# Attention start-up and filler of a fused attention and two-layer network kernel: operands of the second pair, products of zeros, filler rate, copies

## The chip, the cores and the metric

The kernel is one program on one core of a Trainium2 chip. The metric is the device time of one execution in microseconds (us), less being better. TensorE runs the matrix products, VectorE and ScalarE read its results out of PSUM, GpSimd works on SBUF, and SyncE issues most DMAs. The times of three runs and one profiled execution are shown.

## The reference, cut to what matters

```
scores = q @ k.T / 8, masked causally, plus min(-(cum_i - cum_j), 0)   # cum = cumsum(max(s, 0))
attn   = softmax(scores);  x = attn @ v        # batch 4, heads 8, sequence 576, head size 64
x = x.reshape(2304, 512)                       # heads side by side
h = x @ w1_in;  x = (h * sigmoid(1.702 h)) @ w1_out          # 512 -> 2048 -> 512
h = x @ w2_in;  out = (P(h) / Q(h)) @ w2_out                 # P cubic, Q quadratic in |h|
```

## The kernel before, in words

The attention works on one pair of heads at a time: 4 batches of 4 pairs. A pair has five units, blocks of 128 query rows t = 0, 1, 4, 2, 3 (block 4 has 64 rows, both heads together), so there are 80 units; the loop of `attention` (L417) counts them as j. A unit is two `unit_scores` (L251 two products per head; L285 on VectorE adds the mask and takes the minimum, L292 on ScalarE the exponential, L304 on GpSimd scales by the reciprocal sum), and, three units later in the first batch and two later after it, `unit_transpose` (products with the identity, L323 to L344, and a copy `pt<-tp` out of PSUM, L324 to L351) and one unit after that `unit_values` (L370, the product with v).

A pair's operands are made by `prep`, which is a generator in two steps: step one transposes k on TensorE (`tk`, L218), step two q (`tq`); each result is split into a high and a low part (L176 on ScalarE, L179 on VectorE), and the high part is copied to the other half of the partitions by a DMA from SBUF to SBUF (L225, `kh<-kh` and `k<-qs`). The rows with the running sum come by L204 from a scratch in DRAM which `store_sums` fills (L113, L115). The loop takes a step of the next pair's `prep` in a pair's first and second unit; in the very first pair `if j` (L437) holds it back, so there the steps come in units j = 1 and j = 2, and j = 5 is the first unit that needs them. The loads of v are `values` (L152, L156); those of the first two pairs are traced ahead of `store_sums` (L413 to L415).

Until j = 23 there is no other work for TensorE: `fill` (L385) then issues `warm` products of zeros (L75, `idle`), three per unit for j below 4 and one per unit after that. From j = 23 on, `fill` interleaves the first fifth of layer one for the batch that is done (`mlp1_first`, L562 and L586), by a credit of FILL / 20 us per unit in three portions; one batch's work comes to 29.6 us in these costs, so at FILL = 33 it is used up after some 18 units of 20 (L434).

The layer's weights are split into two parts by `convert` (L493 to L506: one DMA, then ScalarE, VectorE, GpSimd in turn). Ten of them are emitted at the units in CONV_J, from j = 9 on; up to j = 23 they share one staging buffer, so that each load waits for the GpSimd sum (L504) of the one before.

TensorE's instructions run in the order written. On the other engines and on SyncE's queue a planner sets the order: it takes, of what it thinks ready, what stands first in the program. `COPY_V` lists the (batch, t) whose copies `pt<-tp` go to VectorE; all others go to ScalarE.

Of the kernel before, what the change touches and what calls it, by code (L numbers as in the profile page):

```python
# [41 lines left out]
PACE = 0.5  # L42
AHEAD_F = (5, 6, 7)
AHEAD_J = (35, 39, 43, 47, 51, 55)
FILL = 33.0
AHEAD, AHEAD_0 = 2, 3
COPY_V = ((0, 0), (0, 4))
W2_SLOTS = 7
CONV_J = (9, 12, 15, 18, 20, 22, 24, 26, 28, 30)
CONV = [(f, 0) for f in range(F1)] + [(f, 1) for f in range(F1)]  # L50
# [5 lines left out]
class Fused:  # L56
# [249 lines left out]
    def unit_transpose(self, att, u):  # L306
# [10 lines left out]
        st["pt"] = {}  # L317
        copy = nc.vector.tensor_copy if (b, t) in COPY_V else nc.scalar.copy
        if t == 4:
# [77 lines left out]
    def attention(self, att, mlp):  # L397
        units = [(b, p, t) for b in range(NB) for p in range(NP) for t in (0, 1, 4, 2, 3)]
        n = len(units)
        self.pairs, self.state = {}, {}  # L400
        self.filler, self.credit = iter(()), 0.0
        self.n_bt = 0
        self.cold, self.idle_bank = True, self.bank("T", "idle")
        self.warm(10)
        nprep = iter(())
        self.sums_load(att)
        ld = self.pair_load(att, 0, 0, True)
        self.sums(att)
        for _ in self.prep(att, 0, 0, ld, True):
            pass  # L410
        start = ld["values"]
        ld = self.pair_load(att, 0, 1)
        start()  # L413
        ld["values"]()
        self.store_sums()  # L415
        done = 0
        for j in range(n + AHEAD + 1):  # L417
            i = max(j - (AHEAD_0 if j < 20 else AHEAD), -1)
            for e in range(done, i):
                for _ in self.unit_transpose(att, units[e]):  # L420
                    pass
                self.unit_values(att, units[e - 1])
            done, k = i + 1, i - 1
            self.stg_free = j > 23
            tr = iter(())
            if j < n:
                b, p, t = units[j]
                idx = j % 5
                if idx == 0 and units[j][1:] != (NP - 1, 0) or (idx == 0 and b + 1 < NB):
                    nprep = self.prep(att, *divmod(b * NP + p + 1, NP), ld)  # L430
            if i >= 0 and i < n and units[i][0] and i % 20 == 1:
                self.filler = chain(self.filler, self.mlp1_first(mlp, units[i][0] - 1))
                self.cold = False
            q = FILL / 20  # L434
            if j < n:
                self.unit_scores(att, units[j], 0)
                if j:  # L437
                    next(nprep, None)
            self.fill(q / 3, 1)
            if 0 <= i < n:  # L440
                tr = self.unit_transpose(att, units[i])
                next(tr, None)
            if j < n:
                self.unit_scores(att, units[j], 1)
            self.fill(q / 3, j < 4)
            for _ in tr:
                pass
            if j < n and idx == 4:
                for _ in nprep:
                    pass  # L450
                g = b * NP + p + 2
                if g < NB * NP:
                    ld = self.pair_load(att, *divmod(g, NP))
                    ld["values"]()
            if k >= 0:
                self.unit_values(att, units[k])
            self.fill(q / 3, j < 4)
            if j == AHEAD_J[0]:
                self.stg_n, self.stg_k = 0, 2
                buf = self.stg_slot[:, 2 * STG : 2 * STG + 1024].bitcast(F32R)  # L460
                buf = buf.rearrange("p (i f) -> p i f", i=2)
                self.queue = [
                    lambda f=f, half=half: self.park(buf, 1, f, half)
                    for f in AHEAD_F for half in range(2)
                ]
            if j in COEF_J:
                with self.behind(self.tail):
                    if j == COEF_J[0]:
                        self.coefficients()
                    else:  # L470
                        self.nc.scalar.activation(self.cf[:, 6:8], self.cf[:, 4:6], AF.Abs)
            if j in CONV_J or j in AHEAD_J:
                with self.behind(self.tail):
                    self.emit(1)
        for _ in self.filler:
            pass
# [434 lines left out]
```

## Time and profile before

| | |
|---|---|
| median of 3 runs | 1064.91 us (1062.8 to 1066.14) |
| profiled execution | 1062.4 us, span 1060.6 us |
| TensorE products (PE) busy | 1029.6 us, 97% |
| VectorE (DVE), ScalarE (ACT), GpSimd (POOL) busy | 805.7 us, 722.8 us, 259.4 us |
| mean granted TensorE clock | 0.993 |

The span is that from the first to the last instruction. The attention ends near 328 us; the rest of the kernel is the two layers. The granted clock is a share of full speed, 1.00 for 2.4 GHz and 0.50 for 1.2 GHz; a stretch in between is a mean of the two.

### The profile page before, as it was taken

What the parts mean: (1) busy time and instruction counts of PE and PEld (TensorE: products, weight loads), DVE (VectorE), ACT (ScalarE), POOL (GpSimd) and SP (SyncE); (2) the same over time, 40 slices, a digit from 0 to 9 for tenths busy, and PEclk for the clock granted to TensorE, in tenths of its full rate; (3) what the DMA queues carried; (4) which work ended last, traced back from release to release, by engine and by line L of the source; (5) the groups of instructions that cost most, each with busy time, mean ns of one, the idle gap of its engine ahead of it and who ended that gap; (6) DMA issues with size and microseconds to landing.
All of it is one profiled execution on the core that took longest, in us unless ns stands there. A gap on an engine that the chain in (4) does not pass through costs nothing.

```text
span 1060.6 us, 19849 instructions
## 1 busy us (share of the span) xinstructions
PE 1029.6 (97%) x7073; PEld 942.3 (89%) x7073; DVE 805.7 (76%) x1874; ACT 722.8 (68%) x1668; POOL 259.4 (24%) x321
## 2 busy tenths in 40 slices
PE   6998999999999999998999999999999999999997
PEld 4767998898999899988999999998999999999996
DVE  6787767766644998884379344898998988989886
ACT  6898868978855675563265224787777777777765
POOL 4455734543420000000000000222222222222222
PEclk8999999999999999999999999999999999999999
DMA  8456455543215648995146546100010010100000
GB/s 183 120 153 163 112 148 157 137 138 82 53 46 222 204 160 277 300 305 175 46 125 209 188 124 243 48 30 30 2 47 14 15 46 1 31 30 1 31 1 30
DMA packets 88203, 117.31 MB, mean 111 GB/s; under 512 B 25728, under 2 KB 71808, under 8 KB 86508
## 3 DMA queue, kind: packets, MB, share of 16 engines
q1 hardware_dynamic: 87688, 115.43, 36.3%
q8 instruction: 56, 0.92, 0.4%
q0 software_dynamic: 192, 0.31, 0.2%
q14 instruction: 43, 0.35, 0.1%
q10 hardware_dynamic: 224, 0.30, 0.1%
HBM read 75.08 MB, written 32.05 MB: 101 GB/s over the span
## 4 chain that ended last, share of the span: by engine, by line
PE 73%; DMA 12%; DVE 6%; ACT 5%; issue 2%; POOL 1%; SPq 0%; ACTq 0%; DVEq 0%; POOLq 0%
PE h L562 29%; PE a L727 18%; PE a L586 12%; DMA raw<-in_moe_w_out_dram 5%; PE s L251 5%; PE O L370 4%; PE tp L344 2%; DMA stgA<-in_moe_w_in_dram 2%; DMA raw<-in_moe_w_in_dram 2%; DMA xp<-x 1%; DVE cvx L504 1%; DMA wd<-park 1%; ACT cvx L499 1%; DVE gl L579 1%; DVE cvx L502 1%
## 5 line engine op out<-in xcount | busy, mean ns | idle before, releaser
L710 POOL TENSOR_TENSOR gl<-u,gh 128x384 fp32r<-128x384 f32 x96 | 105.5, 1099 | 625.9 <-DMA x<-st 339.3
L562 PE MATMUL h<-x,u 128*128 128x288 f32 x1536 | 234.5, 298 | 5.3 <-ACT st L600 1.6
L586 PE MATMUL a<-gh,u 128*128 128x288 f32 x1024 | 232.3, 299 | 4.1 <-DVE st L637 3.0
L562 PEld LDWEIGHTS h<-x,u 128*128 128x128 f32 x1536 | 212.8, 188 | 11.2 <-DVE g L574 3.1
L586 PEld LDWEIGHTS a<-gh,u 128*128 128x128 f32 x1024 | 172.4, 188 | 10.2 <-DVE st L637 2.8
L562 PE MATMUL h<-y,u 128*128 128x384 f32 x864 | 166.2, 336 | 0.0
L562 PEld LDWEIGHTS h<-y,u 128*128 128x128 f32 x864 | 153.0, 188 | 6.3
L586 PE MATMUL a<-gl,u 128*128 128x288 f32 x512 | 148.6, 296 | 1.2 <-DVE gl L579 1.2
L727 PE MATMUL a<-u,gh 128*128 128x512 f32 x432 | 114.9, 394 | 0.9 <-ACT gh L708 0.9
L304 POOL TENSOR_SCALAR bt<-bt,sm 128x128 f32<-128x128 f32 (+3 forms) x129 | 71.3, 563 | 113.8 <-DVE sm L301 59.7
L586 PEld LDWEIGHTS a<-gl,u 128*128 128x128 f32 x512 | 96.3, 188 | 2.6 <-DVE gl L579 1.8
L292 ACT ACTIVATE bt<-bt,mn 128x128 f32<-128x128 f32 (+3 forms) x129 | 74.8, 580 | 29.7 <-DVE mn L285 28.1
L727 PEld LDWEIGHTS a<-u,gh 128*128 128x128 f32 x432 | 80.0, 188 | 14.9 <-ACT gh L708 1.7
L285 DVE CUSTOM_DVE_ANT_0 bt<-s,mask 128x128 f32<-128x128 f32 (+3 forms) x129 | 62.3, 483 | 37.1 <-PE s L251 31.2
L573 ACT ACTIVATE g<-h 128x288 f32<-128x288 f32 x128 | 51.1, 405 | 56.8 <-PE h L562 51.9
L576 ACT ACTIVATE gh<-g 128x288 fp32r<-128x288 f32 x128 | 55.7, 442 | 48.0 <-DVE g L574 47.3
L708 ACT ACTIVATE gh<-u 128x384 fp32r<-128x384 f32 x96 | 50.6, 527 | 54.2 <-DVE u L706 53.2
L693 ACT ACTIVATE y<-h,cf 128x384 f32<-128x384 f32 x96 | 55.6, 579 | 38.6 <-PE h L562 38.6
L574 DVE SCALAR_TENSOR_TENSOR g<-g,h 128x288 f32<-128x288 f32 x128 | 56.9, 448 | 32.4 <-ACT g L573 32.1
L251 PE MATMUL s<-k 68*128 68x256 f32 (+2 forms) x192 | 72.5, 382 | 8.7 <-DVE qs L179 4.8
L698 DVE SCALAR_TENSOR_TENSOR y<-s,cf,y 128x384 f32<-128x384 f32 x96 | 59.4, 618 | 24.5 <-ACT s L695 23.5
L706 DVE SCALAR_TENSOR_TENSOR u<-y,u 128x384 f32<-128x384 f32 x96 | 72.7, 757 | 1.1
(115 smaller groups left out, 2014.5 us busy)
## 6 DMA issues: line engine op xcount, KB each, us to landing
raw<-in_moe_w_in_dram SPq DMA_DIRECT2D x24, 512.0 KB
raw<-in_moe_w_out_dram SPq DMA_DIRECT2D x24, 512.0 KB
x<-st SPq DMA_DIRECT2D x64, 144.0 KB
wd<-park SPq DMA_DIRECT2D x36, 256.0 KB
u<-wd SPq DMA_DIRECT2D x8, 1024.0 KB
x2p<-st SPq DMA_DIRECT2D x32, 144.0 KB
xp<-x2p SPq DMA_DIRECT2D x32, 144.0 KB
xp<-x SPq DMA_DIRECT2D x32, 144.0 KB
```

Source lines behind the costliest of these rows:

```text
L251: nc.tensor.matmul(sc[: c1 - c0, :w], lhsT=q[:, c0:c1], rhs=k[:, j0 : j0 + w], start=m == 0, stop=m == 1,)
L285: nc.vector.tensor_tensor_reduce(bt[:, j0 : j0 + w], sc[:, :w], mask, 1.0, 3.0e38 if i == 0 else mn[:, 0:1], ALU.add, ALU.min, mn[:, i : i ...
L292: ex = nc.scalar.activation(bt[:, :n], bt[:, :n], AF.Exp, bias=mn[:, i : i + 1], scale=-1.0, accum_out=sm[:, col : col + 1],)
L304: nc.gpsimd.tensor_scalar(bt[:, :n], bt[:, :n], inv[:, i : i + 1], 1.0, ALU.mult, ALU.mult)
L562: nc.tensor.matmul(ps_tile, lhsT=u[:, wl, kk * P : (kk + 1) * P], rhs=x(xl, kk), start=(n == 0), stop=(n == 3 * KD - 1),)
L574: nc.vector.scalar_tensor_tensor(g[:, :w], g[:, :w], 1.0, h, ALU.add, ALU.mult)
L576: nc.scalar.activation(gh[:, :w], g[:, :w], AF.Copy)
L586: nc.tensor.matmul(acc, lhsT=u[:, wl, d * P : (d + 1) * P], rhs=g[gl], start=(first and i == 0), stop=(last and i == 2),)
L698: nc.vector.scalar_tensor_tensor(y, s, cf[:, 7:8], y, ALU.mult, ALU.add)
L706: last = nc.vector.scalar_tensor_tensor(p, y, 2.0, p, ALU.subtract, ALU.mult)
L710: nc.gpsimd.tensor_tensor(gl, p, gh.bitcast(F32), ALU.subtract)
L727: nc.tensor.matmul(accs[m], lhsT=g[gl][:, m * P : (m + 1) * P], rhs=u[:, wl, :], start=(f == 0 and i == 0), stop=(f == NF - 1 and i == 2),)
```

## The change

It makes four edits in the attention's loop. `store_sums` is traced ahead of the two loads of v, and the second pair's v is loaded in unit 2. The second pair's `prep` takes its steps in units 0 and 1. The first `fill` of a unit issues its product of zeros only for j below 4 or in a pair's first unit; 15 of the 49 products of zeros go (units 4, 6 to 9, 11 to 14, 16 to 19, 21 and 22). The filler's rate is 30 instead of 33 until j = 43. And in the second batch the copies of t = 0, 1 and 4 go to VectorE.

```diff
-FILL = 33.0
+FILL, FILL_1 = 33.0, 30.0
-COPY_V = ((0, 0), (0, 4))
+COPY_V = ((0, 0), (0, 4), (1, 0), (1, 1), (1, 4))
...
         ld = self.pair_load(att, 0, 1)
+        self.store_sums()
         start()
-        ld["values"]()
-        self.store_sums()
...
-            q = FILL / 20
+            q = (FILL_1 if j < 43 else FILL) / 20
             if j < n:
                 self.unit_scores(att, units[j], 0)
-                if j:
-                    next(nprep, None)
-            self.fill(q / 3, 1)
+                next(nprep, None)
+            self.fill(q / 3, j < 4 or j % 5 == 0)
...
+            if j == 2:
+                ld["values"]()
             if k >= 0:
                 self.unit_values(att, units[k])
```

## Rows read from the trace of the kernel before

**Rows 1.** Windows: stretch, length, busy PE PEld DVE ACT POOL, clock, DMA share, GB/s.
```profile
12.50:27.10 14.60, 11.31 (x60) 8.39 (x60) 9.69 (x36) 8.70 (x26) 2.39 (x5) 0.82 0.77 185
27.10:41.80 14.70, 14.70 (x126) 11.35 (x126) 11.05 (x45) 11.12 (x33) 5.20 (x10) 0.88 0.39 96
41.80:56.30 14.50, 13.33 (x128) 10.28 (x126) 12.07 (x45) 12.88 (x37) 7.71 (x11) 1.00 0.54 142
...
83.90:105.00 21.10, 17.48 (x134) 14.75 (x134) 14.71 (x43) 18.16 (x49) 12.16 (x14) 0.95 0.51 130
105.00:163.00 58.00, 58.00 (x508) 52.39 (x506) 40.19 (x136) 46.33 (x127) 33.36 (x44) 0.99 0.49 128
163.00:171.00 8.00, 8.00 (x90) 6.97 (x89) 7.29 (x25) 7.57 (x23) 3.34 (x5) 1.00 0.71 188
171.00:330.00 159.00, 158.28 (x1422) 142.64 (x1421) 96.90 (x339) 119.11 (x334) 64.74 (x98) 1.00 0.36 95
```

**Rows 2.** Waits of TensorE, 12 to 125 us: total us, times, longest us.
```profile
PE s L251 <- DVE qs L179: 4.8, 1, 4.8
PE s L251 <- DMA k<-qs: 3.3, 1, 3.3
PE tp L344 <- DVE g L574: 1.2, 1, 1.2
PE tp L344 <- ACT pt L348: 1.2, 1, 1.2
PE h L562 <- DVE k L179: 0.9, 1, 0.9
```

**Rows 3.** Timeline of TensorE, second pair's transposes: start us, us.
```profile
15.24 1.16 PE L218 MATMUL tk<-ident,kn 96*128 96x96 f32 x6
...
18.36 0.66 PE L218 MATMUL tq<-ident,qn 96*128 96x96 f32 x6
```

**Rows 4.** Timeline of SyncE's queue, 10 to 22 us: start us, us.
```profile
10.63 0.47 SPq L152 DMA_DIRECT2D vn<-in_v_dram  x1
...
11.87 1.99 SPq L115 DMA_DIRECT2D rows<-stgA  x4
...
21.07 0.49 SPq L225 DMA_DIRECT2D k<-qs  x1
```

**Rows 5.** Windows around the move of q, columns as in rows 1.
```profile
20.00:20.80 0.80, 0.80 (x7) 0.53 (x6) 0.77 (x3) 0.56 (x2) 0.80 (x2) 1.00 0.09 14
20.80:26.00 5.20, 3.00 (x20) 1.74 (x17) 4.07 (x15) 3.77 (x10) 0.77 (x2) 1.00 0.94 234
```

**Rows 6.** DMA issues, 0 to 30 us: count, KB each.
```profile
vn<-in_v_dram SPq DMA_DIRECT2D x4, 128.0 KB
...
k<-qs SPq DMA_DIRECT2D x1, 288.0 KB
```

**Rows 7.** Chain that ended last, in order of time: start us, us, what.
```profile
21.07 5.89 DMA k<-qs
...
32.14 0.22 PE idle L75
...
48.68 5.26 DMA stgA<-in_moe_w_in_dram
```

**Rows 8.** Windows of line 75 alone: length, busy PE, PEld, clock, DMA, GB/s.
```profile
27.10:41.80 14.70, 2.17 (x5) 0.48 (x5) 0.88 0.39 96
```

**Rows 9.** Copies `pt<-tp` by line: ns min/median/max, first and last start.
```profile
L351 DVE COPY pt<-tp x4: 415/418/425, 22.1 to 69.3; 128x256 f32<-128x256 f32 x4
L324 ACT COPY pt<-tp x12: 563/565/591, 91.5 to 319.7; 128x512 f32<-128x512 f32 x12
...
L324 DVE COPY pt<-tp x4: 666/692/693, 29.4 to 72.3; 128x512 f32<-128x512 f32 x4
```

**Rows 10.** Windows after two groups of waits, columns as in rows 1.
```profile
28.00:30.00 2.00, 2.00 (x11) 1.44 (x9) 1.20 (x3) 1.98 (x7) 1.15 (x2) 0.50 0.38 100
...
104.00:106.00 2.00, 2.00 (x10) 1.65 (x11) 1.91 (x8) 1.45 (x5) 2.00 (x4) 0.50 0.88 215
```

## Prediction

> **What bounds the kernel now.** I read the windows by stage first, then TensorE's waits, then the chain of waits, then SyncE's queue and the DMA windows around the one long wait. From 105 us to the end of the attention TensorE is busy all the time: 58.00 of 58.00 us and 158.28 of 159.00 [rows 1]. An edit can win there only by taking products away, and the four edits take none away after unit 22. What can move lies before 105 us. TensorE waits there 4.8 us for the first scores, once 3.3 us for the DMA `k<-qs`, and then in waits of about 1 us [rows 2]. The first is outside the change. The second is its target: unit 5, the second pair's first, is reached at 27.1 - 3.3 = 23.8 us and starts at 27.1, because the move of q issued at 21.07 takes 5.89 us to land [rows 7]. The stage behind it, 27.1 to 41.8, is TensorE's own: 14.70 of 14.70 us [rows 1], and the chain passes through its products, four products of zeros among them (the first stands in [rows 7]). From about 43 us on the chain passes no longer through TensorE but through the conversions of the weights: a load, ScalarE, VectorE, GpSimd, the next load, one in about 10 us, five of them up to 90 us (the first load stands in rows 7). ScalarE is busy for 12.88 of 14.50 us there and TensorE waits at times [rows 1]. So three resources hand over: DMA until 27, TensorE until 42, conversions and ScalarE until 103, and TensorE from there on.
>
> **The change, part by part.**
>
> The stall at unit 5. k's and q's transposes go from 15.24 and 18.36 [rows 3] to one unit sooner each, after the first scores of units 0 and 1; units there last 2 to 3 us, so the move of q can be issued at about 19 instead of 21. But issuing is only half: the move takes 5.89 us because of what is in the queue ahead of it. The DMA engines are 94% busy at 234 GB/s from 20.8 to 26.0 [rows 5], which is 1.22 MB, or four pieces of 288 KB [rows 6]: k and q of the fourth pair and the two moves. All came through SyncE's one queue, and I take it that they drain in about the order of issue. So I estimate the landing by the drain. The queue had a hole from 20.0 to 20.8 (9% busy, [rows 5]), which an earlier move fills: -0.8. `store_sums` (issued at 11.87) takes the place of the last two loads of the second pair's v, from 10.63 [rows 4]: everything that waits for the stored rows can go 1.24 us sooner. Those v loads, 128 KB and a small rest [rows 6], are now drained after it: at 220 GB/s some +0.7. Sum: 26.96 - 0.8 - 1.2 + 0.7 = 25.6, and the end of the stall goes from 27.1 to 25.7: **-1.4 us**. Bounds: the whole 3.3 (the moves pass the fourth pair's loads, 2 x 1.3 us, and land before TensorE is there) to +1.3 (all 288 KB of v stand ahead of the move and nothing else goes sooner). What the sooner transposes cost TensorE is nothing: the same 12 products, in units 0 and 1 instead of 1 and 2. On ScalarE and VectorE eight splits come ahead of the exponentials of units 1 and 2; there ScalarE is busy for 8.70 of 14.60 us [rows 1], which is cover enough; without it the exponentials come 2 us late, still ahead of their transposes three units on.
>
> The clock after it. After this stall the granted clock falls: 0.50 from 28 to 30 [rows 10], and 0.88 as a mean over the second pair against 1.00 in the third [rows 1]. The second pair takes 14.70 us without a wait; the third is busy for 13.33. The difference, 1.4 us, is the price. After a single wait of 1.2 us (for `pt`, at 46 us [rows 2]; the stretch is at 1.00 [rows 1]) the clock did not fall; after 1.2 and 0.9 close together (at 100 and 102 us [rows 2]) it did: 0.50 from 104 to 106 [rows 10]. A stall of 2.0 us lies between these rows in kind: longer than the one, but with solid work on both sides, unlike the other. I take that it does not fall: **-1.4**, bounds 0 and -1.7 (3.4 us at half clock).
>
> The products of zeros. Of the 15, the one in unit 4 lies just before the stall and is worth nothing. Those of units 6 to 9 lie on the chain, 0.22 to 0.23 us each (first in [rows 7]; the stage has 5 in 2.17 us of overlapping durations [rows 8], of which the one in unit 5 stays): **-0.9**. The other ten lie where the conversions and ScalarE set the pace: TensorE comes sooner and waits longer. I take **0**; bounds -2.2 (all ten at 0.22) and, if the clock falls in the longer waits, a price of 1.7 for each fall.
>
> The Trainium skill, page TensorE: Matmul & The Clock Gate, section What's actually happening, says that slow is the engine's default and that activity releases it. It speaks against this edit: the zeros are activity. By the trace both falls came after over 2 us of waits and none after 1.2; by the rule each longer wait is a candidate, and one fall in each of four stretches would turn the sum about. That is a rival below.
>
> Filler at 30. A unit from 23 to 42 gets 1.50 instead of 1.65 us. In 83.9 to 105, where TensorE waits for others (17.48 of 21.10, [rows 1]), five units put 0.75 us less into the waits; that work is done later, on the chain: 0 to +0.75. In 163 to 171 before, two units had no filler and TensorE was still full, 8.00 of 8.00 [rows 1]: there is no hole for the rest to fill. Value 0, with the copies.
>
> The copies. Per pair one of 256 columns, two of 512 and a small one leave ScalarE and cost VectorE 0.42 + 2 x 0.69 = 1.8 us and a little [rows 9]. From 105 on both are below TensorE (40.19 and 46.33 of 58.00, [rows 1]): nothing either way. Before, only the second batch's first pair counts: ScalarE loses 2 x 0.56 and a shorter copy, some 1.5 of 18.16 us, in 83.9 to 105; VectorE gains some 2 on 14.71. Waits for either engine occur there [rows 2], so -1.5 to +2; it cancels with the filler's share, and I take **0** for the two.
>
> Sum: -1.4 - 1.4 - 0.9 = **-3.7 us**. ScalarE can follow it (11.12 busy of 14.70 in the second pair), and the first conversion, whose weights were loaded long before, moves with unit 9, so that the chain of conversions starts sooner by it. Behind 105 us all follows: TensorE is the bound, and the weights of the second stage are loaded into space which the attention gives back. The profiled execution took 1062.4 us (span 1060.6), 2.5 under the median of 1064.9; its own sum would be 1058.7. The metric's median is what I predict: 1064.9 - 3.7 = **1061.2**.
>
> **The rivals.**
>
> No gain at the start: the stores, v and the fourth pair's loads refill the queue, so that the move of q lands at 26 to 27 as before (for: DMA 94% busy; against: the hole, and 1.2 us sooner on SyncE), and the clock falls as before. Left are 0.9 for the zeros, of which ScalarE may eat half: -0.5, **1064.4**. Chance 0.21. That the edit does not do what it says is the same case.
>
> All gain: the moves pass the fourth pair's loads. -3.3 - 1.4 - 0.9, and half of the ten zeros where TensorE still is the slowest: -1.1; together -6.7, **1058.2**. For it: both moves stand ahead of those loads in the program; against: the loads were ready sooner in the order before. Chance 0.18.
>
> Slower: without the zeros the clock falls in the second to fourth pair and once at 85 us, where waits of 0.5 to 1.2 us lie. A fall is 3.4 us at half clock, 1.7 us. The stall's and the zeros' 2.3 us are gone from the second fall on; with four falls it is 6.8 - 2.3 = +4.5, **1069.4**. Against: at half clock the stage would still be partly covered by ScalarE, and the 1.2 us wait did not bring a fall. Chance 0.14.
>
> VectorE late: its copies stand behind the doubled conversions near 100 us, where TensorE already waits for it (1.2 + 0.9, [rows 2]): +2, and half of the start's gain lost: 1065 to 1067. Chance 0.05.
>
> The forecast itself has 0.42, with a range of its own from 1059.5 to 1063.
>
> **How the numbers follow.** A measurement of this kernel can tell 0.3%, 3.2 us, from no change: 1061.7 to 1068.1 is the same. The forecast gives 0.27 to faster and 0.15 to same, the second rival 0.18 to faster, the first 0.20 to same and 0.01 to slower, the third 0.14 to slower, the fourth 0.02 to same and 0.03 to slower. Together: faster 0.45, same 0.37, slower 0.18. The range is 1057 to 1067.5: it takes in the full gain and the first and fourth rival, and leaves out the four falls.
>
> **What would show it.** In the profile after, the wait of `s` for `k<-qs` should be near 2 us, with the move issued near 19; if it is 3 or more, the first step is wrong, if it is gone, the second rival holds. The clock in the second pair should be 1.00, or the second step is wrong. The second pair should take about 12.5 us in place of 14.7. The loads of the conversions should begin some 3.7 us sooner, in steps of 10 us as before; if the steps shrink, the ten zeros counted. A clock below 1.00 between 35 and 100 us would speak for the third rival, longer waits for VectorE near 100 us for the fourth.

## The result

The changed kernel takes 1068.6 us (median of 16 runs) beside 1064.2 us of the kernel before (16 runs on the same chip): a ratio of 1.0053, 95% interval 1.0038 to 1.0068. It is slower by 0.5%; the forecast was 1061.2 us, faster. It went the other way, and lies above the range (1057 to 1067.5).

TensorE's clock has a share in it. Each run comes with its mean granted clock; one minus it, times the time, is called the clock loss from here on. It is half of the time at half clock, whether TensorE had work in it or not. It is 12.0 us as a mean over the 16 runs of the changed kernel (standard error 1.0), and 7.7 us over the 138 runs of the kernel before that were made beside the kernels below (0.2). The difference of 4.3 us is as large as the time lost, but not all of it is time: from run to run, 1 us more of clock loss goes with 0.43 us more of time in the changed kernel (standard error 0.17) and with 0.63 in the kernel before (0.07). An estimate by these slopes gives the clock 1.8 to 2.7 us of the 4.4.

The first profile of the changed kernel is of 1067.2 us (span 1065.4), and by the clock the best of its runs: 0.995. Its clock is better than in the profile of the kernel before (0.993, span 1060.6), and still it is 4.8 us longer. So it shows the new waits and a loss that is not the clock's.

Windows by stage of the changed kernel, columns as in [rows 1]:

```profile
12.50:27.10 14.60, 10.92 (x59) 7.80 (x59) 10.30 (x40) 10.14 (x31) 3.54 (x7) 0.88 0.80 184
27.10:41.80 14.70, 13.30 (x117) 11.12 (x118) 9.36 (x38) 9.87 (x29) 3.75 (x7) 0.88 0.34 82
41.80:56.30 14.50, 12.90 (x124) 10.02 (x122) 13.13 (x48) 12.26 (x34) 7.59 (x11) 1.00 0.55 144
83.90:105.00 21.10, 16.57 (x139) 13.73 (x140) 15.90 (x49) 16.04 (x44) 12.17 (x16) 1.00 0.59 120
105.00:163.00 58.00, 56.93 (x490) 50.67 (x489) 47.76 (x148) 43.13 (x119) 34.17 (x42) 0.97 0.53 142
163.00:171.00 8.00, 8.00 (x87) 7.53 (x85) 7.30 (x25) 7.61 (x23) 5.08 (x6) 1.00 0.47 114
171.00:330.00 159.00, 158.30 (x1425) 142.86 (x1423) 98.03 (x343) 120.08 (x338) 64.77 (x98) 1.00 0.37 98
```

The second pair's stage, full before (14.70 of 14.70), now has 1.4 us of idle TensorE and the same clock, 0.88. From 105 to 163 us TensorE does 490 products where it did 508.

TensorE's waits, 12 to 125 us, beside [rows 2]:

```profile
PE s L251 <- ACT k L176: 4.1, 1, 4.1
PE tq L218 <- DVE mn L285: 2.9, 1, 2.9
PE s L251 <- DMA k<-qs: 2.9, 1, 2.9
PE tp L344 <- ACT pt L348: 2.6, 2, 1.4
PE tp L344 <- DVE mn L285: 1.6, 1, 1.6
PE tp L344 <- POOL bt L304: 1.4, 2, 0.8
PE tp L323 <- POOL stgA L304: 1.0, 1, 1.0
```

The wait for `k<-qs` is still there, 2.9 us after 3.3. The waits behind it are more and longer than before. The row that matters below is 1.6 us for `mn` (L285): before, no wait between 41 and 84 us was longer than 1.2.

SyncE's queue up to the move of q, beside [rows 4], and the chain, beside [rows 7]:

```profile
10.22 2.03 SPq L115 DMA_DIRECT2D rows<-stgA  x4
12.29 0.42 SPq L152 DMA_DIRECT2D vn<-in_v_dram  x1
12.76 0.68 SPq L156 DMA_DIRECT2D vn<-in_v_dram  x1
...
14.45 0.33 SPq L145 DMA_DIRECT2D kn<-in_k_dram  x1
14.83 0.44 SPq L145 DMA_DIRECT2D qn<-in_q_dram  x1
15.31 0.44 SPq L145 DMA_DIRECT2D kn<-in_k_dram  x1
15.80 0.45 SPq L493 DMA_DIRECT2D stgA<-in_moe_w_in_dram  x1
16.92 0.54 SPq L225 DMA_DIRECT2D kh<-kh  x1
17.83 0.31 SPq L145 DMA_DIRECT2D qn<-in_q_dram  x1
...
20.06 0.49 SPq L225 DMA_DIRECT2D k<-qs  x1
```

```profile
20.06 6.87 DMA k<-qs
51.03 4.56 DMA stgA<-in_moe_w_in_dram
...
83.34 7.74 DMA stgA<-in_moe_w_in_dram
```

k and q of the second pair are transposed one unit sooner than in [rows 3], as planned:

```profile
13.96 1.16 PE L218 MATMUL tk<-ident,kn 96*128 96x96 f32 x6
17.08 0.71 PE L218 MATMUL tq<-ident,qn 96*128 96x96 f32 x6
```

The move of q is issued at 20.06 instead of 21.07 and takes 6.87 us instead of 5.89: it lands at 26.93, before at 26.96. Both loads of the fourth pair and the weights of a conversion went out ahead of it, as they did before. The chain's loads of weights begin later, too: 51.03 instead of 48.68.

### The profile page after: what moved, and what is told of

Its sections match the earlier page's. It is cut to its first block, busy times and chain, and to the rows that moved or that the text cites. A ratio compares the mean times of both kernels' runs of the same rounds, so it can differ in the third digit from the quotient of the medians.

```text
span 1065.4 us, 19815 instructions
## 1 busy us (share of the span) xinstructions
PE 1028.7 (97%) x7058; PEld 941.4 (88%) x7058; DVE 814.4 (76%) x1890; ACT 717.5 (67%) x1652; POOL 259.8 (24%) x321
## 4 chain that ended last, share of the span: by engine, by line
PE 72%; DMA 11%; DVE 8%; ACT 6%; issue 2%; SPq 1%; POOL 1%; ACTq 0%; DVEq 0%; POOLq 0%
PE h L562 28%; PE a L727 18%; PE a L586 11%; DMA raw<-in_moe_w_out_dram 7%; PE s L251 5%; PE O L370 4%; PE tp L344 3%; DMA stgA<-in_moe_w_in_dram 2%; DMA raw<-in_moe_w_in_dram 1%; DVE cvx L504 1%; ACT cvx L499 1%; DVE cvx L502 1%; PE idle L75 1%; DVE g L574 1%; DMA k<-qs 1%
## 5 line engine op out<-in xcount | busy, mean ns | idle before, releaser
L562 PEld LDWEIGHTS h<-x,u 128*128 128x128 f32 x1536 | 212.4, 188 | 10.8 <-DVE g L574 4.6
L285 DVE CUSTOM_DVE_ANT_0 bt<-s,mask 128x128 f32<-128x128 f32 (+3 forms) x129 | 62.2, 483 | 31.4 <-PE s L251 23.2
```

The source lines that it names most:

```text
L285: nc.vector.tensor_tensor_reduce(bt[:, j0 : j0 + w], sc[:, :w], mask, 1.0, 3.0e38 if i == 0 else mn[:, 0:1], ALU.add, ALU.min, mn[:, i : i ...
L562: nc.tensor.matmul(ps_tile, lhsT=u[:, wl, kk * P : (kk + 1) * P], rhs=x(xl, kk), start=(n == 0), stop=(n == 3 * KD - 1),)
```

## The experiments

Each kernel ran in five rounds beside the kernel before on the same chip, two further profiles of the whole change apart. Theory K says that the time goes where TensorE waits long enough for its clock to fall; theory R, that any edit here gives the other engines a new order, and that a new order costs some us whatever the edit was. All results in one table (times in us; loss is the clock loss; the last column has the falls of the clock to 0.50 that begin between 41 and 84 us in one profile; the profile of the kernel before has none):

| kernel | median | ratio to before (95%) | loss | falls |
|---|---|---|---|---|
| whole change | 1068.6 | 1.0053 (1.0038 to 1.0068) | 12.0 | 0, 1, 1 |
| start_alone | 1062.7 | 1.0005 (0.9986 to 1.0023) | 6.7 | 0 |
| zeros_alone | 1066.0 | 1.0025 (1.0008 to 1.0042) | 10.8 | 1 |
| rate_alone | 1066.2 | 1.0028 (1.0011 to 1.0045) | 10.4 | 0 |
| copies_alone | 1062.2 | 0.9992 (0.9975 to 1.0009) | 6.8 | 1 |
| rate_up36 | 1069.8 | 1.0062 (1.0044 to 1.0080) | 10.2 | 0 |
| rate_early30 | 1067.7 | 1.0030 (1.0007 to 1.0052) | 9.8 | 0 |
| zeros_conv_sooner | 1067.4 | 1.0034 (1.0015 to 1.0052) | 12.8 | 2 |
| zeros_twice | 1067.9 | 1.0033 (1.0017 to 1.0049) | 7.9 | 0 |
| start_and_copies | 1065.1 | 1.0021 (1.0002 to 1.0040) | 8.0 | 0 |
| rate_fed | 1064.5 | 1.0021 (1.0004 to 1.0038) | 8.3 | 0 |
| zeros_back | 1065.6 | 1.0024 (1.0005 to 1.0044) | 7.1 | 0 |
| zeros_back_41 | 1063.9 | 1.0002 (0.9984 to 1.0019) | 8.0 | 1 |
| rate_back | 1069.8 | 1.0065 (1.0040 to 1.0090) | 12.9 | 1 |
| before_fed | 1063.2 | 0.9996 (0.9977 to 1.0016) | 7.2 | 0 |
| zeros_first | 1064.6 | 1.0009 (0.9988 to 1.0029) | 9.5 | 1 |
| zeros_later | 1064.5 | 1.0019 (1.0000 to 1.0037) | 8.2 | 0 |

The rows are of 12 runs each, but 16 for the whole change and 6 for rate_up36 and rate_back. The losses have standard errors of 0.5 to 1.1 us (rate_back 1.8). The loss of start_alone leaves out its profiled run, whose records show 0.95 from end to end at no longer a time.

**The four edits one by one.** In these expectations R looks at the conversions of the weights, which a new order brings later, and its rival V puts the loss down to the copies on VectorE near 100 us. The diff of the change, cut in four: `store_sums` and `prep` sooner (start_alone); the condition of `fill` (zeros_alone); FILL_1 (rate_alone); COPY_V (copies_alone).

> Only the first edit: store_sums ahead of the loads of v, the second pair's v in unit 2, its operands begun in unit 0. Theory R (the loss comes from the planned orders that change when the products of zeros go, so that the conversions of the weights run late): this alone is within 1 us of the kernel before, since the move of q again lands near 27 us. Theory V (the loss is VectorE's, from its three more copies per pair): the same, within 1 us. A third, that the start itself costs: 2 to 5 us slower, the first scores or unit 5 later than 12.5 and 27.1 us.

> Only the second edit: products of zeros only below unit 4 and at new pairs. Theory R: 3 to 5 us slower, with the third and later loads of the conversions (68.7, 78.6 us before) several us late and the clock still at 1.00 from 35 to 100 us. Theory V: 0 to 2 us faster. If the clock is what the zeros hold, it is slower and the granted clock is below 1.00 in the second to fourth pair.

> Only the third edit: filler at 30 instead of 33 until unit 43. Both theories R and V: within 1 us of the kernel before. If less filler in the waits is the cause, 1 to 3 us slower, with more waiting of TensorE from 84 to 105 us.

> Only the fourth edit: copies of t = 0, 1, 4 of the second batch on VectorE. Theory V: 3 to 5 us slower, with waits of TensorE for VectorE of 3 us or more in all between 95 and 130 us. Theory R: within 1.5 us of the kernel before, because VectorE is late only when the conversions pile up there.

V falls: the start and the copies are level with before; the zeros and the rate each cost 2.5 to 3 us, and the clock loss rises with just these two (10.8 and 10.4 after 7.5 in the same rounds). R missed too: it had the rate level, and the clock at 1.00 without the zeros. The rate came out as the third case of its expectation had it: TensorE waits 4.6 us between 84 and 105 us, before 3.6. And copies_alone, with all its zeros, has a fall at 61 us in its profile and is level all the same. The fall that zeros_alone adds is this (timeline of TensorE, then windows, columns as in [rows 1]):

```profile
46.72 0.52 PE L344 MATMUL tp<-ident,bt 128*128 128x128 f32 x3 [1.60 <-DVE mn L285]
```

```profile
46.00:48.00 2.00, 1.28 (x23) 1.05 (x23) 1.94 (x7) 1.98 (x7) 0.20 (x1) 0.98 0.31 114
48.00:50.00 2.00, 2.00 (x13) 1.85 (x9) 1.91 (x9) 1.95 (x6) 1.79 (x3) 0.50 0.66 142
50.00:52.00 2.00, 2.00 (x16) 1.78 (x16) 1.52 (x6) 1.00 (x4) 1.76 (x3) 0.66 0.77 184
```

It is the same 1.60 us for `mn` as in the changed kernel, and 13 and 16 products run where 23 ran.

**The rate up, and down in the early units alone.**

```diff
-            q = FILL / 20
+            q = (36.0 if j < 43 else FILL) / 20      # rate_up36
+            q = (30.0 if j < 31 else FILL) / 20      # rate_early30
```

> Before with one edit: the filler's rate is 36 instead of 33 until j = 43 (the change had 30). Theory K (TensorE's clock: the time is lost where TensorE waits for others long enough for the granted clock to fall; less filler in those waits means more falls): more filler in the waits from 84 to 125 us, so the mean clock over the runs is at or above before's (loss 7.5 us or less, by one minus the mean clock times the time) and the time is 0 to 3 us below before. Theory R (any change of the filler's amounts makes the planner set the other engines' orders anew, and a new order costs a few us by chance): anything from 3 us below to 3 us above, with no tie to the rate's sign; above by 2 us or more speaks for R.

> Before with the filler's rate at 30 only for j below 31 (the eight units in 79 to 105 us) and 33 from there on. Theory K: the whole loss of the rate edit comes from these units, where TensorE waits; the time is 2 to 3 us above before (1.002 to 1.003) and the mean clock lower than before's by some 0.003, as with the rate edit alone. Theory L (filler that is done late costs its own time, since TensorE is full from 105 us on): the eight units put off 8 x 0.15 = 1.2 us, so at most 1.2 us above before, and no lower clock.

Both cost time: the rate has no direction in which it gains, which is R's forecast and not K's. For the rate up, one place can be seen, and it is of K's kind, a wait and half clock. The filler outruns the conversions, and TensorE waits at 130 and 132 us for a second half of weights, then runs at half clock:

```profile
130.35 0.40 PE L586 MATMUL a<-gh,u 128*128 128x288 f32 x1 [0.61 <-ACT u L505]
132.21 0.85 PE L586 MATMUL a<-gh,u 128*128 128x288 f32 x2 [1.33 <-POOL u L506]
```

```profile
132.00:134.00 2.00, 1.79 (x7) 1.79 (x8) 0.46 (x1) 0.00 (x0) 0.15 (x1) 0.50 0.60 177
134.00:136.00 2.00, 2.00 (x11) 1.95 (x10) 0.32 (x1) 0.37 (x1) 0.00 (x0) 0.50 0.27 82
```

The rate at 30 in the early units alone costs 3.2 us, as much as over all units; its interval (0.7 to 5.5 us) still touches the 1.2 that theory L allowed, but the clock loss, 9.8 after 8.0 in the same rounds, went K's way, by 0.0017 of the clock where K said 0.003.

**Conversions sooner, and more zeros.**

```diff
-CONV_J = (9, 12, 15, 18, 20, 22, 24, 26, 28, 30)
+CONV_J = (8, 11, 14, 17, 20, 22, 24, 26, 28, 30)   # zeros_conv_sooner, on zeros_alone
-            self.fill(q / 3, 1)
+            self.fill(q / 3, 1 if j < 4 else 2)        # zeros_twice, on before
```

> The zeros edit alone (products of zeros after unit 3 only at new pairs), and the first four conversions emitted one unit sooner (CONV_J 8, 11, 14, 17 in place of 9, 12, 15, 18), so that the planner has them ahead of that unit's softmax. The zeros edit alone measured 1066.0, before 1063.7. Theory C (without the zeros the planner sets softmax work between the steps of the conversions, the weights come 4 us late, 82.72 instead of 78.63 us for the fourth load, and TensorE waits for it): the loads come 2 to 4 us sooner again and the time goes back to 1063 to 1064.5, the clock with it. Theory Z (the zeros themselves keep TensorE's clock from falling, wherever the conversions stand): the time stays at 1065.5 to 1067 and the mean clock stays near 0.990.

> Before with two products of zeros in place of one in the first fill of units 4 to 22 (19 more, 0.22 us each). Theory Z (the zeros hold the clock up): the mean clock rises above before's 0.993 (loss below 6 us), and the time is from 2 us below to 1 us above before, the products on the chain at units 6 to 9 costing 0.9. Theory C (only the order of the conversions counts): the clock stays where it was within 0.0015, and the time follows the loads of the weights: with the fourth issued near 78.6 us it is 0.5 to 2 us above before, with it at 82 us or later 2 to 4 us above.

In zeros_alone the loads of weights had come late, as in the changed kernel. The first fence is zeros_alone, the second zeros_conv_sooner:

```profile
49.12 0.38 SPq L493 DMA_DIRECT2D stgA<-in_moe_w_in_dram  x1
...
82.72 0.39 SPq L493 DMA_DIRECT2D stgA<-in_moe_w_in_dram  x1
```

```profile
45.93 0.38 SPq L493 DMA_DIRECT2D stgA<-in_moe_w_in_dram  x1
...
79.45 0.38 SPq L493 DMA_DIRECT2D stgA<-in_moe_w_in_dram  x1
```

They came 3.2 and 3.3 us sooner again (before, the second of the two is at 78.63), and the time did not come back, nor the clock (12.8). So theory C falls: late weights are a companion of the loss, not its cause. The time, 1067.4, is just above theory Z's 1067. Twice the zeros leave the clock where it was (7.9) and cost 3.5 us, 19 products of 0.22 us being 4.2. Here theory Z missed, which had the loss below 6 us: zeros beyond those of before bring no clock, and are only work.

**The two level edits together, and zeros in the late waits.**

```diff
+            if 23 <= j < 31:          # rate_fed, on rate_alone; before_fed, on before
+                self.warm(1)
```

> The change without its zeros edit and without its rate edit: the two edits of the start and the copies together. Theory K (the whole of the loss is in the zeros and the rate edits, through clock falls and waits of TensorE in 45 to 125 us): 1061 to 1064, mean clock 0.993 as before. Theory R (any other order costs a few us against the order before): 1065 to 1068 although both edits alone were level.

> The rate edit alone, and one product of zeros more in each of the units 23 to 30 (8, 0.22 us each), in the stretch 79 to 105 us where TensorE waits for others. The rate edit alone measured 1066.2 at a mean clock of 0.9902. Theory K by the products themselves (less work in the waits lets the clock fall): the clock comes back to 0.9925 or more and the time to 1063 to 1065. Theory R: the clock stays at 0.9885 to 0.9915 and the time within 1065 to 1069, the zeros being work added.

The start and the copies together are 2 us slower (1.0002 to 1.0040) though level alone, at the clock of before: this is R's forecast, not K's. rate_fed brought the clock loss from 10.4 to 8.3 (standard error of the difference 1.0), close to what K asked for, and the time into K's span; its ratio, 1.0021, is too near that of rate_alone, 1.0028, to be told from it.

**Two further profiles of the changed kernel.**

> The changed kernel, a second profile. Its runs lost 12.0 us to the clock as a mean (one minus the mean clock, times the time; before 7.5), its first profile only 5.1, with the same three falls as before (12, 28 and 104 us). Theory K: this profile has one to three falls more, of about 1.7 us each, behind waits of TensorE between 40 and 140 us. Theory R: no more falls than before, and the time lies in waits without a fall.

> The changed kernel, a third profile; the same is expected as of the second. By theory K the places of the falls differ from execution to execution, since waits of 1 to 3 us near the limit bring one or don't; by theory R they stay at 12, 28 and 104 us.

They took 1073.0 and 1071.4 us. The falls that the first profile lacked are there, at differing places. All three executions have the wait of 1.60 us for `mn`. Here it is in the second, and the windows behind it:

```profile
53.52 0.52 PE L344 MATMUL tp<-ident,bt 128*128 128x128 f32 x3 [1.60 <-DVE mn L285]
```

```profile
54.00:56.00 2.00, 2.00 (x25) 1.73 (x25) 1.91 (x7) 1.95 (x6) 1.05 (x1) 0.60 0.28 62
56.00:58.00 2.00, 2.00 (x10) 1.95 (x9) 1.60 (x7) 1.57 (x5) 1.73 (x5) 0.50 0.66 137
58.00:60.00 2.00, 2.00 (x16) 1.65 (x16) 1.22 (x4) 0.95 (x3) 1.38 (x2) 0.50 1.04 288
```

and in the third, where it brought nothing at once and the clock fell only after the waits of the next pair, at 64 us:

```profile
48.34 0.52 PE L344 MATMUL tp<-ident,bt 128*128 128x128 f32 x3 [1.60 <-DVE mn L285]
```

```profile
48.00:50.00 2.00, 1.66 (x25) 1.38 (x26) 1.94 (x7) 1.95 (x7) 0.22 (x1) 1.00 0.15 55
...
64.00:66.00 2.00, 1.97 (x24) 1.60 (x25) 1.87 (x7) 1.90 (x7) 1.85 (x2) 0.68 0.90 302
66.00:68.00 2.00, 2.00 (x9) 1.95 (x10) 1.37 (x5) 1.95 (x6) 1.45 (x4) 0.50 1.03 212
```

One program, one wait, and in one execution a fall, in another none. The runs of the changed kernel scatter from 1065.1 to 1075.0, and those of before no less: the 138 runs go from 1058.5 to 1070.0.

**One costly edit taken out of the whole, and the same zeros in the kernel before.**

```diff
-            self.fill(q / 3, j < 4 or j % 5 == 0)
+            self.fill(q / 3, 1)                                  # zeros_back
+            self.fill(q / 3, j < 4 or j >= 10 or j % 5 == 0)     # zeros_back_41
-            q = (FILL_1 if j < 43 else FILL) / 20
+            q = FILL / 20                                        # rate_back
```

> The whole change without its zeros edit (all 49 products of zeros stand). Theory Z (the zeros held the clock in the waits of the second to fourth pair): the loss to the clock falls from 12.0 to 9 us or less, no fall between 41 and 84 us in the profile, and the time is 2 to 4 us below the whole change, 1064.5 to 1066.5 against 1064.2 of before. Theory R (the order): the clock's loss stays at 11 us or more, or the time stays within 1 us of the whole change.

> The whole change with the zeros of units 10 to 22 put back (41 to 79 us; only those of units 4 and 6 to 9 are gone, which the forecast counted at 0.9 us of gain). Theory Z: as with all zeros back, the loss to the clock at 9 us or less and the time 2 to 4 us below the whole change; if the zeros of units 6 to 9 are a gain as the forecast had it, 0.5 to 1 us below the run with all zeros back. Theory R: within 1 us of the whole change, or above.

> The whole change with the filler's rate at 33 throughout. Theory K: the rate's share of the loss comes back, some 2 to 3 us below the whole change (1065.5 to 1066.5 against 1064.2), its loss to the clock 9 to 10 us, and the falls between 41 and 84 us stay, as the zeros are gone. Theory R: no tie to the edit; anywhere from 1064 to 1071.

> Before with one product of zeros more in each of the units 23 to 30 (79 to 105 us). Theory K by the products: the fall at 102 to 106 us goes or shortens, the loss to the clock 6 to 7 us, the time 0.5 to 2 us below before. Theory R: 1 to 4 us above before. If neither, level: the zeros lie in waits, and the waits of 1 us that bring the fall are at other places.

The zeros put back bring the clock loss from 12.0 to 7.1 and 8.0 and the time down by 3.1 and 4.7 us, both inside theory Z's span or below it. The rate put back brings nothing (12.9), where K had 2 to 3 us. In the whole change, then, the loss to the clock goes with the zeros edit. Not all of the time does: zeros_back is still 2.6 us above before (0.5 to 4.7) at the clock of before. TensorE between 41 and 84 us, one fence each for before, the second profile of the changed kernel, zeros_back, and the first profile of the changed kernel (columns as in [rows 1]):

```profile
41.00:84.00 43.00, 39.66 (x370) 29.74 (x369) 37.45 (x136) 38.90 (x108) 24.42 (x34) 1.00 0.64 171
```

```profile
41.00:84.00 43.00, 39.56 (x334) 30.92 (x337) 34.03 (x123) 33.55 (x91) 20.88 (x30) 0.88 0.47 117
```

```profile
41.00:84.00 43.00, 39.52 (x367) 30.05 (x373) 38.20 (x138) 38.72 (x109) 23.76 (x32) 1.00 0.62 169
```

```profile
41.00:84.00 43.00, 36.56 (x341) 27.85 (x339) 36.62 (x128) 37.07 (x104) 22.85 (x32) 1.00 0.57 149
```

In the first three the busy time is equal and the clock is not. The products (370, 334, 367, 341) do not measure the clock: ten of those missing are the zeros themselves, and the first profile has 341 at full clock. before_fed is level, which neither K nor R had: its late fall, at 105 us, stayed.

**Which zeros.**

```diff
-            self.fill(q / 3, 1)
+            self.fill(q / 3, j < 4 or j >= 10 or j % 5 == 0)   # zeros_first: without units 4, 6 to 9
+            self.fill(q / 3, j < 10 or j % 5 == 0)             # zeros_later: without 11 to 14, 16 to 19, 21, 22
```

> Before without the products of zeros of units 4 and 6 to 9 (24 to 41 us); those of units 10 to 22 stay. Forecast's third step: 0.9 us below before (0.9992). Theory Z (zeros matter where TensorE waits): the loss to the clock stays at 7 to 8.5 us, the time is 0 to 1 us below before. Theory R (another order of the planner): 1 to 4 us above.

> Before without the products of zeros of units 11 to 14, 16 to 19, 21 and 22 (41 to 79 us); those of units 4 to 9 stay. Forecast: no change. Theory Z: the loss to the clock at 10.5 us or more and the time 2 to 4 us above before, as with the whole zeros edit. Theory R: the time above before by some us, too, but the loss to the clock at 9 us or less.

Here theory Z missed. The early zeros alone were not the safe ones to take (loss 9.5, standard error 0.8, and no gain), and the later ones alone did not bring the loss of the clock (8.2), though some 2 us of time: that is R's forecast. In the whole change the same ten later zeros, put back, brought clock and time back (zeros_back_41). Which zeros hold the clock, and whether it is they that do, is not settled.

## Why the prediction was wrong

None of the three gains in the sum came as time, and two terms that were set at 0 had a cost: the ten later zeros and, by itself, the filler's rate.

**The stall at unit 5 (forecast -1.4).** What came was the first rival. The forecast took the hole in the DMA at 20.0 us, and 1.2 us on SyncE, as time won by the move of q. The same loads as before stood ahead of the move, at 14.45 to 17.83 us: two of k, two of q and one of weights, of the third and fourth pair and of a conversion. They went sooner too, and filled the hole (392 GB/s from 20.0 to 20.8, before 14). The move was issued at 20.06, not near 19, and its end came at the same time. That is no chance of one execution: unit 5 starts at 26.75 to 28.52 us (mean 27.4) in the eight profiles with this edit, and at 26.95 to 27.55 (mean 27.2) in the twelve without it. Nor is it the bulk of the move, which lands in sixteen parts: the trace has them from 25.15 to 26.93 us, half of them by 25.6; before, from 25.68 to 26.96, half by 26.4. Most of it came sooner and the last part did not; why, stays open. The stall was 2.9, 3.4 and 3.0 us in three profiles, and 2.6 in start_alone; before, 3.3.

**The clock behind it (forecast -1.4).** It fell as before [rows 10], as the stall stayed:

```profile
28.00:30.00 2.00, 2.00 (x11) 1.78 (x10) 0.19 (x1) 1.21 (x4) 0.00 (x0) 0.50 0.23 40
```

The forecast's condition was sound: in copies_alone, rate_alone and before_fed TensorE came to unit 5 later, the stall was 1.8 to 2.3 us, and no fall came. There the stretch from the third pair's first transposes of k to the fourth's takes 13.2 us, before 14.7: a fall costs 1.5 us here, and the size was right too. After the sixteen stalls of 2.8 us or more a fall came, with one exception, zeros_first (start_alone's records do not tell):

```profile
27.42 0.36 PE L251 MATMUL s<-k 68*128 68x256 f32 x1 [3.23 <-DMA k<-qs]
```

```profile
28.00:30.00 2.00, 2.00 (x22) 1.56 (x20) 1.60 (x8) 1.75 (x6) 1.16 (x2) 1.00 0.25 48
```

**The four zeros of units 6 to 9 (forecast -0.9).** They are gone, one product of zeros being left in the stage where [rows 8] has five, but TensorE gave the time to a wait for a copy on ScalarE. The first fence is the window of line 75 alone, the second the timeline:

```profile
27.10:41.80 14.70, 0.63 (x1) 0.15 (x1) 0.88 0.34 82
```


```profile
34.13 0.52 PE L344 MATMUL tp<-ident,bt 128*128 128x128 f32 x3 [1.40 <-ACT pt L348]
```

The reason given against this, that ScalarE has room with 11.12 us busy of 14.70, is the step that failed: a busy share below one does not say that the copy is early. From the third pair's transposes of k to the fourth's the changed kernel takes 15.4 us and zeros_back, with the zeros, 15.6. Without the start edit the gain is there at first: 13.9 us in zeros_alone against 14.7 before, with a fall each. It does not last: the next pair takes 15.7 after 14.6, and zeros_first shows no gain in the whole, 1.0009 (0.9988 to 1.0029).

**The other ten zeros (forecast 0).** This is the step that went furthest wrong in the whole change. The forecast said that TensorE comes sooner and waits longer there, which is what happened, and priced it at nothing. With all fifteen zeros put back the time is 3.1 us lower, with these ten alone 4.7. The third rival had the right price of a short fall, 1.7 us, but its time, 1069.4, is near the measured one in part by luck: it wanted four falls more, and the three profiles show none, one (and a longer one at unit 5), and two. The argument that held its chance down, that a wait of 1.2 us had not brought a fall, spoke of the waits that before has. Without the zeros a wait of 1.6 us and others of 1.0 and 0.8 came, and the clock fell after some of them in some executions. The Trainium skill, page TensorE: Matmul & The Clock Gate, section What's actually happening, says that activity releases the engine from its slow state. The trace agrees in part: four kernels with all fifteen zeros gone lose 10.8 to 12.9 us to the clock, and before and zeros_back 7.7 and 7.1; but three with all zeros and another rate lose 9.8 to 10.4, and zeros_later, without these ten, 8.2. So it is not shown that the products themselves hold the clock, and not the order of the other engines which comes with them: zeros in the late waits brought rate_alone's loss down as well, zeros_later speaks against it, and no run parts the two.

**The filler at 30 (forecast 0).** Alone it costs 3.0 us (1.0011 to 1.0045), four times the bound of 0.75 that was set. In the whole change, putting it back gains nothing (1.0065 after 1.0053, within the error). That the forecast summed its terms is not what failed: the four edits alone make 0.0005 + 0.0025 + 0.0028 - 0.0008 = 0.0050, and the whole 0.0053. The rate alone does not fit such a sum, 0.0028 by itself and -0.0012 in the whole, a difference of 0.0040 with an error of 0.0034. The 2 us of start and copies together are within the error of their sum.

**The copies (forecast 0).** Right by themselves: 0.9992 (0.9975 to 1.0009). In the changed kernel VectorE is busier, 47.76 us after 40.19 from 105 to 163, and TensorE's longest new wait, 2.9 us at 101.5, is for it; what that costs there no run tells.

What stays open: why a new rate costs 3.0 to 6.6 us in either direction, and start with copies 2 us (0.2 to 4.3); and what the changed kernel loses beside the clock, 4.8 us in its first profile. Of the sixteen other kernels near the one before none is faster than it by more than its interval; start_alone, copies_alone, before_fed, zeros_back_41 and zeros_first are level with it, and by this R's claim, that a new order costs time whatever the edit was, does not hold for all.

## What to carry to other kernels

A product of zeros in a stretch where TensorE waits may not be idle work: ask what the clock does without it, in many executions, before taking it out. A transfer that is issued sooner gains nothing where the loads ahead of it only go sooner with it: what counts is the landing of its last part. Where a planner sets the order of four engines, run small edits one by one, then together, and put each back alone: most costs added up here within their errors, that of the rate did not.

## What was not expected of the hardware

The same wait of 1.60 us, at the same place of the same program, is followed by half clock in one execution and by full clock in two others. A fall mostly lasts 3 to 7 us. In zeros_later it lasted 10 us, and in the second profile of the changed kernel, after a stall of 3.4 us, from 28 to 44 us with TensorE busy for 15.3 of the 16:

```profile
34.00:36.00 2.00, 1.33 (x7) 1.06 (x6) 1.66 (x5) 1.93 (x6) 0.59 (x2) 0.50 0.49 136
...
42.00:44.00 2.00, 2.00 (x14) 1.67 (x13) 0.00 (x0) 1.26 (x3) 0.00 (x0) 0.50 0.00 0
```

And one profile can miss the effect: the changed kernel's first lost 5.1 us to the clock up to 120 us, its next two 17.1 and 10.2.
